# Rotary attention and a SiLU feed-forward layer on one core: small steps on three engines, and a new order of the work

## The chip, the cores and the metric

The kernel runs on one NeuronCore of one Trainium2 chip. The metric is device time in microseconds (us), from the start to the end of one execution. The kernel before takes 629.87 us (median of 3 runs, 629.48 to 632.24).

## What is computed

```python
def _attn_ref(q, k, v):                       # 4 batches, 8 heads, 576 positions, 64 numbers each, float32
    q_rot, k_rot = rotate(q), rotate(k)       # rotary embedding with cos and sin of 576 x 32 angles
    scores = (1 / 8) * q_rot @ k_rot.T
    attn = softmax(scores)                    # per row, minus its maximum
    return attn @ v

def _moe_ref(x, w_in, w_out):                 # x: 2304 x 512; w_in: 512 x 2048; w_out: 2048 x 512
    h = x @ w_in
    return (h * sigmoid(h)) @ w_out
```

`x` is the output of the attention, with the eight heads side by side. The scores of batch 0 are computed in float32; almost everything else is split into two float16 parts, a high one and a low one, whose products TensorE adds up.

## The kernel before, in words

**Stages.** The work is cut into some 2,500 named parts. Attention goes by *slots* `S i` (144 of them): the scores of up to 128 query rows of one head against all 576 keys. A slot has matmuls into PSUM (`S`, L953 for the first 16 slots, L1072 and L1081 for the others), the row maximum on VectorE (`max`, L958, L1102, L1104, L1097), the exponential on ScalarE (`exp`, L961 or L1115), the reciprocal of its sum (`nr1`, L1129), the split into a high part (`hi`, by `part_hi`, L324 or L330) and a low part (`lo`, by `part_lo`, L336 or L339) and a transposing DMA. In the first 16 slots there is no split: TensorE transposes the exponentials back into the slot's own PSUM buffer (`ET`, L966) and an engine copies them out (`EV`, L973), which sets that PSUM buffer free. Batch 0's q and k come into the same PSUM buffers by TensorE transposes (`qP`, L479 to L489) and are copied out by `qE` (L501, or L324 on VectorE). Tag `s` has two such buffers, `s3` one more.

Then `pv` multiplies by v, and the result is x for one *unit* (256 tokens; eight units and a rest). The feed-forward layer goes in *steps* over one unit and one of eight pieces `i` of the 2048 hidden columns: `m1` (24 matmuls, L1238), `tanh` on ScalarE (L1250), `g` on VectorE (L1254), its split `gh` and `gl`, and `m2` (twice 6 matmuls, L1295). `m1` has one PSUM buffer, so the next `m1` waits for this `g`.

**Weights.** Piece `i` of w_in and w_out (`wld`, L777 and L783) lands as float32 in a place that is still free, among others in `ring`. Three rounding steps follow (`wT` L798, `wC` L803 or L805, `wX` L811), the sum of squares (`wtr`, L839 on ScalarE or L349 on TensorE, `wtd` L353, `wmm` L854), the scale, and the split (`whi`, `wlo`) into w16.

**Scales.** `add_scale` (L297) makes every scale in three VectorE instructions on a tile of 128 x 1, 2 or 5: `sc0` (L305) takes the exponent bits, `sc1` (L311) multiplies them into a power of two `inv`, and `sc2` (L317) is its reciprocal `s`. There are 36 scales: 8 of weights, 12 of q and k, 16 of v. `add_w_group` (L880) makes a group's constants for unit 0, which runs over the weights in three groups (2, 3 and 3 pieces) as they come in: `wgr`, with two or three products, a maximum and a reciprocal (L892 to L894), all on VectorE. `tanh` of unit 0 reads what it makes. `times` (L323) is the helper for a product.

**Order.** Nothing is scheduled by the machine: `ORDER` names every part by its number and gives the engine that runs it (`a` ScalarE, `d` VectorE, `p` GpSimd, `t` TensorE, `s` SP's DMA queue), and `Plan.run` (L180) issues them so. Each engine executes its instructions in that order, and an instruction that waits holds up all that stand behind it on its engine.

Of the kernel before, what the change touches and what calls it, by code (L numbers as in the profile page):

```python
# [11 lines left out]
I32 = mybir.dt.int32  # L12
# [26 lines left out]
3s 472s 474p 473a 2s 1s 4s 9p 10p 475d 478a 468s 469a 11t 0d 6d 12d 5p 7t 8a 470d 471d 476a 663t 664d 673t 665a 479d  # L39
13s 477d 480t 481d 482d 20s 22p 674d 675a 14t 15d 21p 23t 45s 24a 36s 61s 483d 676t 677a 666t 667a 38d 484a 52s 25p  # L40
678t 26d 679d 680a 37p 39t 46t 42p 486a 485d 27t 28a 41d 488s 47d 489a 681t 682a 40a 54d 62t 487d 490a 57p 63d 29s 43t
668t 669d 496s 683t 44a 19s 497a 492s 58p 30t 53p 35s 670a 671t 684d 685a 75s 672a 31d 68t 491d 500a 69d 494a 70d 493a
501d 498d 71d 16p 499d 32d 74s 495d 686t 18d 687a 502a 503d 64d 55t 34d 504t 688t 693t 73s 48a 50d 56a 505d 506d 507d
1875d 689d 514s 694d 76a 690a 698t 695a 691t 692a 510d 696t 699d 534s 516d 508p 59t 60d 700a 701t 77a 697d 78t 509d
708t 702a 515a 79d 84p 713t 709d 714d 703t 1878t 536a 535a 512a 511p 704d 710a 705a 652d 90p 711t 91p 92p 518s 715a
517d 706t 562s 712a 707a 520a 519a 1876t 723t 718t 724d 513p 716t 717a 719d 563a 564a 1877d 538s 521d 565d 66d 539a
85p 86p 1885t 524t 725a 540a 537d 726t 727a 541d 80d 1879d 522t 1880p 523d 542t 543d 525d 720a 1889d 721t 1881p 558s
526t 544a 527d 81d 545d 546t 547d 1882d 728t 722a 559a 554s 560p 528d 561d 738t 529d 555a 548d 556a 733t 1883t 729d
# [1361 lines left out]
```

## Time and profile before

| | |
|---|---|
| median of 3 runs | 629.87 us |
| the profiled execution | 631.0 us, of which span 629.2 us |
| PE busy | 595.4 us (95%) |
| DVE busy | 468.0 us (74%) |
| ACT busy | 401.2 us (64%) |
| POOL busy | 323.5 us (51%) |
| mean granted clock of TensorE | 0.972 of 2.4 GHz |

In the profile PE is TensorE, PEld its weight loads, DVE VectorE, ACT ScalarE, POOL GpSimd and SP the engine that issues most DMAs. The shares are averages over stages that differ: VectorE is at 74% of the span, but at 95% in the stage in which the last weights come in. So the profile is read stage by stage. A granted clock of 1.00 is 2.4 GHz and 0.50 is 1.2 GHz.

### The profile page before, as it was taken

What the parts mean: (1) busy time and instruction counts of PE and PEld (TensorE: products, weight loads), DVE (VectorE), ACT (ScalarE), POOL (GpSimd) and SP (SyncE); (2) the same over time, 40 slices, a digit from 0 to 9 for tenths busy, and PEclk for the clock granted to TensorE, in tenths of its full rate; (3) what the DMA queues carried; (4) which work ended last, traced back from release to release, by engine and by line L of the source; (5) the groups of instructions that cost most, each with busy time, mean ns of one, the idle gap of its engine ahead of it and who ended that gap; (6) DMA issues with size and microseconds to landing.
All of it is one profiled execution on the core that took longest, in us unless ns stands there. A gap on an engine that the chain in (4) does not pass through costs nothing. (4 is left out here: it accounts for less than half of the span.)

```text
span 629.2 us, 12529 instructions
## 1 busy us (share of the span) xinstructions
PE 595.4 (95%) x4484; PEld 396.9 (63%) x4484; DVE 468.0 (74%) x1062; ACT 401.2 (64%) x834; POOL 323.5 (51%) x304
## 2 busy tenths in 40 slices
PE   1879999889999999999999999999999999999997
PEld 1657675555566666666667666567566666666663
DVE  2747879999998998999899999898778765121222
ACT  2656979988978777777676578577655653221221
POOL 4635636545665674745747654567674443423210
PEclk9976969989999999999999999999999999999999
DMA  6677708899989969998985889798866576100101
GB/s 200 180 257 272 239 1 205 232 207 188 193 149 185 195 123 157 175 187 181 201 147 127 150 167 166 128 197 160 160 111 115 99 124 95 42 10 1 35 1 33
DMA packets 210670, 91.17 MB, mean 145 GB/s; under 512 B 188464, under 2 KB 194352, under 8 KB 210608
## 3 DMA queue, kind: packets, MB, share of 16 engines
q1 hardware_dynamic: 210288, 89.79, 68.7%
q10 hardware_dynamic: 320, 0.59, 0.5%
q8 instruction: 35, 0.57, 0.4%
q14 instruction: 27, 0.22, 0.1%
HBM read 36.73 MB, written 4.72 MB: 66 GB/s over the span
## 5 line engine op out<-in xcount | busy, mean ns | idle before, releaser
L1238 PEld LDWEIGHTS <-w_in 128*128 128x128 f16 x1728 | 167.3, 98 | 37.1 <-issue 7.5
L1238 PE MATMUL m<-xh,w_in 128*128 128x256 f16 x1024 | 180.2, 274 | 1.3 <-DVE g L1254 1.2
L1295 PE MATMUL m<-w_out,gh 128*128 128x512 f16 x576 | 171.5, 379 | 0.0
L1238 PE MATMUL m<-xl,w_in 128*128 128x256 f16 x512 | 140.3, 274 | 0.6 <-POOL xl L1043 0.5
L1115 ACT ACTIVATE e<-s,small 128x576 f32<-128x576 f32 x128 | 98.8, 773 | 41.6 <-DVE pn L336 9.8
L1295 PE MATMUL m<-w_out,gl 128*128 128x512 f16 x288 | 109.1, 379 | 0.0
L1254 DVE SCALAR_TENSOR_TENSOR g<-g,m 128x512 f32<-128x512 f32 x72 | 49.0, 680 | 71.0 <-ACT g L1250 42.2
L1295 PEld LDWEIGHTS <-gh 128*128 128x128 f16 x576 | 52.6, 99 | 54.9 <-issue 4.0
L336 DVE SCALAR_TENSOR_TENSOR pn<-e,small,pn 128x576 f16<-128x576 f32 x85 | 77.4, 914 | 7.3 <-POOL pn L324 3.6
L1250 ACT ACTIVATE g<-m,small 128x512 f32<-128x512 f32 x64 | 43.7, 682 | 49.8 <-PE m L1238 43.0
L324 POOL TENSOR_SCALAR e<-e,small 128x576 f32<-128x576 f32 x43 | 37.5, 872 | 57.5 <-ACT pn L330 25.0
L1081 PE MATMUL s<-Tk,Tq 128*128 128x512 f16 (+1 forms) x384 | 59.9, 286 | 0.7 <-ACT e L1115 0.7
L339 POOL TENSOR_TENSOR pn<-e,pn 128x576 f16<-128x576 f32 x43 | 58.5, 1360 | 3.6
L324 POOL TENSOR_SCALAR pn<-e,small 128x576 f16<-128x576 f32 x40 | 36.6, 914 | 46.2 <-DVE small L1129 31.0
L330 ACT ACTIVATE pn<-e,small 128x576 f16<-128x576 f32 x65 | 49.8, 768 | 16.4 <-DVE small L1129 8.4
L1183 PE MATMUL pv<-pt,vh 128*64 128x320 f16 (+1 forms) x504 | 54.1, 290 | 0.0
L1295 PEld LDWEIGHTS <-gl 128*128 128x128 f16 x288 | 28.1, 98 | 34.0
L1097 DVE TENSOR_SCALAR_CACHE_REDUCE s<-s,small 128x576 f32<-128x576 f32 x57 | 46.1, 815 | 2.4 <-PE s L1087 1.2
L336 DVE SCALAR_TENSOR_TENSOR gl<-g,small,gh 128x512 f16<-128x512 f32 x50 | 41.1, 823 | 5.6 <-ACT gh L330 3.7
L1081 PEld LDWEIGHTS <-Tq 128*128 128x128 f16 x384 | 28.7, 100 | 25.3 <-issue 2.9
L1104 DVE TENSOR_REDUCE small<-s 128x1 f32<-128x576 f32 x51 | 38.0, 747 | 5.4 <-PE s L1081 4.4
L330 ACT ACTIVATE gh<-g,small 128x512 f16<-128x512 f32 x44 | 31.5, 716 | 14.5 <-DVE g L1254 13.1
(205 smaller groups left out, 1030.9 us busy)
## 6 DMA issues: line engine op xcount, KB each, us to landing
w_out<-in_moe_w_out_dram SPq DMA_DIRECT2D x4, 1024.0 KB, 7.6
w_in<-in_moe_w_in_dram SPq DMA_DIRECT2D x4, 1024.0 KB, 6.1
out_dram<-ob SPq DMA_DIRECT2D x28, 128.0 KB, 2.4
io<-in_q_dram SPq DMA_DIRECT2D x12, 288.0 KB, 3.3
io<-in_k_dram SPq DMA_DIRECT2D x12, 288.0 KB, 3.6
io<-in_v_dram SPq DMA_DIRECT2D x12, 288.0 KB, 4.0
io<-in_v_dram SPq DMA_DIRECT2D x13, 256.0 KB, 4.4
ring<-in_moe_w_in_dram SPq DMA_DIRECT2D x3, 1024.0 KB, 7.8
```

The source lines that it names most:

```text
L324: e.tensor_scalar(out=out, in0=in0, scalar1=s1, scalar2=s2, op0=ALU.mult, op1=ALU.bypass if s2 is None else ALU.mult)
L330: act.activation(hi, src, AF.Copy, scale=s)
L336: dve.scalar_tensor_tensor(out=lo, in0=src, scalar=s, in1=hi, op0=ALU.mult, op1=ALU.subtract)
L339: e.tensor_tensor(out=lo, in0=src, in1=hi, op=ALU.subtract)
L1081: pe.matmul(o, tq[:, j, 2 * c:2 * c + 2, :], kt[:, r0:r1, js], start=(n == 0), stop=(n == 1))
L1097: dve.tensor_scalar(out=t, in0=t, scalar1=cc[1], scalar2=None, op0=ALU.mult, op1=ALU.min, accum_out=m_of(1, 2),)
L1115: act.activation(buf("e", i), buf("s", i)[:, 0:S], AF.Exp, bias=m_of(1, 2), scale=-1.0 if fused[i] else cc[0], accum_out=m_of(2, 3),)
L1183: pe.matmul(o[64 * j:64 * j + 64, 0:m], vt[part][:, j, s, :], pt[:, a, j, 0:m], start=(z == 0), stop=(z == len(steps) - 1),)
L1238: pe.matmul(t[:, c, 0:n], w[:, wz, kk, fs], xx[:, kk, 0:n], start=(kk == 0 and x == 0), stop=(kk == KD - 1 and x == 2),)
L1250: act.activation(g[:, :, 0:n], t[:, :, 0:n], AF.Tanh, scale=th_v[units[u][0]][:, i:i + 1])
L1254: dve.scalar_tensor_tensor(out=g, in0=g, scalar=1.0, in1=t, op0=ALU.add, op1=ALU.mult)
L1295: pe.matmul(o, gs[gz][:, c, ts], w[:, wz, c], start=(first and c == 0 and x == 0), stop=(last and c == 1 and x == 2),)
```

## The change

Four edits:

- `sc1` may run on VectorE or GpSimd, `sc2` on VectorE, GpSimd or ScalarE, `wgr` on VectorE or GpSimd.
- The reciprocals of powers of two in `sc2` and `wgr` become integer arithmetic on the bits: 254 x 2^23 minus the bits (`flip`). The maximum in `wgr` becomes a two-operand instruction on GpSimd.
- `ORDER` is another table. By engine: of 36 `sc1`, 17 are on VectorE and 19 on GpSimd; of 36 `sc2`, 11 on VectorE, 14 on GpSimd, 11 on ScalarE; all three `wgr` on GpSimd, six instructions each. Larger parts change engine too, among them `rope` (rotary products, 53 on GpSimd and 35 on VectorE before, 39 and 49 now), `lo` (43 on GpSimd and 85 on VectorE before, 35 and 93 now), `hi` (65 on ScalarE, 40 on GpSimd, 23 on VectorE before, 75, 31 and 22 now) and `xh` (24 on ScalarE, 6 on VectorE, 2 on GpSimd before, 17, 14 and 1 now).
- Every part is still there once; TensorE's count of matmuls is the same.

```diff
 ORDER = """
-3s 472s 474p 473a 2s 1s 4s 9p 10p 475d 478a 468s 469a 11t 0d 6d 12d 5p 7t 8a 470d 471d 476a 663t 664d 673t 665a 479d
...
 """
-        def f1():
-            dve.tensor_scalar(
+        def f1(e):
+            eng[e].tensor_scalar(
                 out=inv, in0=live["bits", it].bitcast(F32), scalar1=2.0 ** 50, scalar2=2.0 ** -70,
                 op0=ALU.mult, op1=ALU.max,
             )
-        def f2():
-            dve.reciprocal(out=s, in_=inv)
+        def f2(e):
+            flip(e, s, inv)
         add("sc0", key, "d", f0, deps, list(bufs) + [bb], it)
-        add("sc1", key, "d", f1, [("sc0",) + key], [bb], it)
-        return add("sc2", key, "d", f2, [("sc1",) + key], (), it)
+        add("sc1", key, "dp", f1, [("sc0",) + key], [bb], it)
+        return add("sc2", key, "dpa", f2, [("sc1",) + key], (), it)
+
+    def flip(e, out, in_):
+        o, x, c = out.bitcast(I32), in_.bitcast(I32), float(254 << 23)
+        if e == "a":
+            act.activation(o, x, AF.Copy, scale=-1.0, bias=c)
+        else:
+            eng[e].tensor_scalar(out=o, in0=x, scalar1=-1.0, scalar2=c, op0=ALU.mult, op1=ALU.add)
...
-        def f():
-            times(dve, th_v[0][:, ii], inv_w[:, ii, 0], vn[0]["inv"], 2.0 ** -9)
+        def f(e):
+            e_ = eng[e]
+            times(e_, th_v[0][:, ii], inv_w[:, ii, 0], vn[0]["inv"], 2.0 ** -9)
...
-                dve.tensor_tensor(out=r, in0=inv_w[:, ii, 0], in1=inv_w[:, ii, 1], op=ALU.mult)
-                dve.reduce_max(out=r_g, in_=r, axis=AX.X)
-                dve.reciprocal(out=t, in_=r_g)
-                times(dve, alpha_g[:, ii], r, t, 2.0 ** -16)
-            times(dve, c_st[:, z:z + 1], r_g, vn[0]["inv"], 0.5)
-        add("wgr", (z,), "d", f, ...)
+                e_.tensor_tensor(out=r, in0=inv_w[:, ii, 0], in1=inv_w[:, ii, 1], op=ALU.mult)
+                if e == "d":
+                    e_.tensor_reduce(out=r_g, in_=r, axis=AX.X, op=ALU.max)
+                else:
+                    e_.tensor_scalar(
+                        out=r_g, in0=r[:, 0:1], scalar1=r[:, 1:2], scalar2=r[:, n - 1:n], op0=ALU.max, op1=ALU.max
+                    )
+                flip(e, t, r_g)
+                times(e_, alpha_g[:, ii], r, t, 2.0 ** -16)
+            times(e_, c_st[:, z:z + 1], r_g, vn[0]["inv"], 0.5)
+        add("wgr", (z,), "dp", f, ...)
```

**ScalarE, early in the program.** `pt<-s` is an `EV`, `Tk<-s` and `Tq<-s3` are `qE`, and `ring<-ring` is the rounding of a piece of the weights that has just landed. Line numbers after the change are up to 14 higher. Before:

```order
L501 ACTIVATE Tq_360<-s3_347 128x576
L798 ACTIVATE ring_133<-ring_133 128x1024
L973 ACTIVATE pt_284<-s_308 128x5x128
L501 ACTIVATE Tk_375<-s_322 128x576
L803 ACTIVATE ring_133<-ring_133 128x1024
```

With the change:

```order
L975 ACTIVATE e_343,small_118<-s_319,small_118 128x576
L509 ACTIVATE Tk_365<-s_352 128x576
L811 ACTIVATE ring_133<-ring_133 128x1024
L987 ACTIVATE pt_292<-s_319 128x5x128
L806 ACTIVATE ring_133<-ring_133 128x1024
```

Before, the copies out of both `s` buffers (`pt<-s_308`, `Tk<-s_322`) stand behind the instruction that waits for the ring's load; now `Tk<-s_352` stands ahead of it and only `pt<-s_319` behind it.

**TensorE, at the same place.** `s_410` and `s_454` are slot 1, `s_416` and `s_421` slot 4; `pv<-w_out` are matmuls for v's sum of squares. Before:

```order
L489 MATMUL s3_397<-id_t_125,n_341 64x128
L489 MATMUL s3_397<-id_t_125,rt_362 64x128
L953 MATMUL s_410<-Tk_203,Tq_184 128x64 x2
L953 MATMUL s_410<-Tk_203,Tq_184 128x448
L953 MATMUL s_416<-Tk_266,Tq_360 128x64 x2
L953 MATMUL s_416<-Tk_266,Tq_360 128x448
L349 LDWEIGHTS w_out_120
```

With the change:

```order
L497 MATMUL s3_403<-id_t_125,n_374 64x128
L497 MATMUL s3_403<-id_t_125,rt_394 64x128
L967 MATMUL s_421<-Tk_290,Tq_367 128x64 x2
L967 MATMUL s_421<-Tk_290,Tq_367 128x448
L357 LDWEIGHTS w_out_120
```

Slot 4 has moved ahead of slot 1, and v's five matmuls between them; slot 4 takes the buffer that `Tk<-s_352` frees.

**SP, the first issues.** Before:

```order
L423 DMA id_t_125<-in_ident_dram 128x128
L783 DMA w_out_120<-in_moe_w_out_dram 128x2x1024
L412 DMA cos_t_123<-in_cos_dram 128x128 x2
L414 DMA cos_t_123<-in_cos_dram 64x32 x2
L412 DMA sin_t_124<-in_sin_dram 128x256 x2
L414 DMA sin_t_124<-in_sin_dram 64x64 x2
L440 DMA w_in_119<-in_q_dram 128x2x256
```

With the change:

```order
L785 DMA w_in_119<-in_moe_w_in_dram 128x4x512
L448 DMA w_in_119<-in_q_dram 128x2x256
L453 DMA w_in_119<-in_q_dram 64x64 x2
L448 DMA w_in_119<-in_k_dram 128x2x256
L453 DMA w_in_119<-in_k_dram 64x64 x2
L420 DMA sin_t_124<-in_sin_dram 128x256 x2
L422 DMA sin_t_124<-in_sin_dram 64x64 x2
L431 DMA id_t_125<-in_ident_dram 128x128
L420 DMA cos_t_123<-in_cos_dram 128x128 x2
L422 DMA cos_t_123<-in_cos_dram 64x32 x2
L791 DMA w_out_120<-in_moe_w_out_dram 128x2x1024
```

The first piece of w_out has moved from the second place to behind q, k, sin, the identity and cos.

## Rows read from the trace of the kernel before

**Rows 1.** The page: the span, and the busy time of each engine.

```profile
span 629.2 us, 12529 instructions
PE 595.4 (95%) x4484; PEld 396.9 (63%) x4484; DVE 468.0 (74%) x1062; ACT 401.2 (64%) x834; POOL 323.5 (51%) x304
```

**Rows 2.** Busy time by stage; PEclk is the granted clock; last DMA share, GB/s.

```profile
0.00:38.00 38.00, 17.68 (x122) 13.84 (x123) 18.06 (x34) 15.80 (x23) 22.07 (x38) 1.00 0.72 215
38.00:58.50 20.50, 20.43 (x79) 15.74 (x79) 12.69 (x26) 13.34 (x28) 5.88 (x6) 0.50 0.60 209
58.50:79.00 20.50, 19.73 (x149) 14.27 (x148) 15.53 (x35) 19.48 (x33) 12.88 (x11) 1.00 0.83 273
79.00:89.30 10.30, 10.30 (x44) 8.26 (x45) 6.56 (x18) 6.80 (x13) 2.53 (x3) 0.50 0.01 2
...
99.40:165.70 66.30, 61.19 (x410) 37.39 (x406) 63.34 (x144) 58.27 (x110) 35.94 (x29) 0.97 0.90 202
165.70:578.80 413.10, 410.70 (x3314) 271.95 (x3313) 329.08 (x771) 267.39 (x579) 232.11 (x208) 1.00 0.76 139
578.80:629.20 50.40, 45.70 (x306) 29.65 (x304) 13.73 (x21) 10.56 (x34) 8.45 (x10) 0.99 0.09 22
```

**Rows 3.** The waits of PE up to 166 us: total, times, longest (us).

```profile
PE s L479 <- POOL n L465: 13.7, 1, 13.7
PE s L953 <- ACT pt L973: 3.5, 2, 3.3
...
PE pv L666 <- DVE small L305: 1.5, 1, 1.5
```

**Rows 4.** The timeline at 29 to 43 us, of SP's queue, ACT and PE.

```profile
29.32 1.38 SPq L777 DMA_DIRECT2D ring<-in_moe_w_in_dram  x1
...
36.02 1.12 ACT L798 ACTIVATE ring<-ring 128x1024 f32<-128x1024 f32 x1 [4.92 <-DMA ring<-in_moe_w_in_dram]
37.03 0.69 ACT L973 ACTIVATE pt<-s 128x640 f32<-128x640 f32 x1
...
37.78 4.84 PE L953 MATMUL s<-Tk,Tq 64*128 64x64 f32 x12 [3.32 <-ACT pt L973]
```

**Rows 5.** The timeline of the first two weight issues and the first use of w_out.

```profile
1.18 0.42 SPq L783 DMA_DIRECT2D w_out<-in_moe_w_out_dram  x1
...
6.82 1.15 ACT L798 ACTIVATE w_out<-w_out 128x1024 f32<-128x1024 f32 x1 [4.80 <-DMA w_out<-in_moe_w_out_dram]
...
10.91 0.59 SPq L777 DMA_DIRECT2D w_in<-in_moe_w_in_dram  x1
```

**Rows 6.** Groups of small instructions: count, busy us, mean ns, idle before.

```profile
L311 DVE TENSOR_SCALAR small<-small 128x2 f32<-128x2 f32 (+2 forms) x36 | 8.2, 231 | 0.4
L317 DVE RECIPROCAL small<-small 128x2 f32<-128x2 f32 (+2 forms) x36 | 5.8, 160 | 0.5
L1122 ACT ACTIVATE small<-small 128x1 f32<-128x1 f32 x69 | 13.4, 197 | 0.9
L1385 POOL MEMSET const-float32-1.0<- 128x1 f32 x1 | 0.1, 99 | 0.0
L467 POOL TENSOR_TENSOR rt<-w_in,sin_t 128x64 f32<-128x64 f32 x3 | 1.0, 321 | 0.0
```

**Rows 7.** The timeline of `wgr` on DVE: its first and its last instruction.

```profile
104.93 0.22 DVE L324 TENSOR_SCALAR small<-small 128x3 f32<-128x3 f32 x1
...
105.64 0.34 DVE L324 TENSOR_SCALAR small<-small 128x3 f32<-128x3 f32 x2
```

**Rows 8.** Instructions that write `pn`: duration in ns, least, median, largest.

```profile
L336 DVE SCALAR_TENSOR_TENSOR pn<-e,small,pn x85: 794/815/2035, 101.6 to 525.5; 128x576 f16<-128x576 f32 x85
...
L324 POOL TENSOR_SCALAR pn<-e,small x40: 739/748/1877, 103.3 to 523.5; 128x576 f16<-128x576 f32 x40
```

**Rows 9.** Groups of the `rope` products on POOL and on DVE.

```profile
L561 POOL TENSOR_TENSOR rt<-io,sin_t 128x576 f32<-128x576 f32 x15 | 24.7, 1656 | 8.8 <-DVE io L568 3.2 <-DMA io<-in_k_dram 3.0 <-PE s L489 1.4
...
L568 DVE TENSOR_TENSOR io<-io,rt 128x576 f32<-128x576 f32 x11 | 9.3, 848 | 0.0
```

More of the change, by code (lines that the diff above doesn't have):

```diff
@@ L44 @@
[L44 to L48, printed above, removed]
@@ new lines @@
+2352a 2345t 1778d 1754d 1755d 1779a 1780d 2346a 1703s 2353d 1771a 1781d 1741D 1758t 1759d 2348t 1756p 1742a 2358t
+1757s 1743a 2354p 1782d 1783d 2355p 1785t 1786d 2359a 2360d 1787a 1744a 1772d 1745d 2349a 1975t 2365t 2361a 1976d
+1760a 1746p 1747d 1761a 1784s 1773a 1803t 1748s 2362p 2356t 2357t 1762a 1763d 1977d 2366a 1788a 2367d 1804D 1774p
+1775s 1794t 2372t 1805d 1764d 2350s 1765d 1789d 1766s 1795d 1796a 1806a 1790d 1791a 1792d 1793s 1807a 1808d 1830t
+2363t 2364t 2368p 1797a 2369p 1831D 2373a 1798d 1799d 1809a 1810p 1800d 1811s 1821t 1822D 1823d 1832a 1833a 1848t
@@ new lines @@
+2370t 1978t 1824a 1849D 2374d 1801p 1825d 1826d 2375a 1827d 1828p 1979a 1866t 1850a 1851a 2379t 1867D 1868a 2376d
+1852a 1802s 1869a 1853d 1829s 1854d 2380a 1855p 1870d 1871d 1856s 1872a 1812t 1873p 2371t 1874s 1839t 1813d 1814d
+1815a 1816a 2381d 1840d 2382p 2377t 2378t 1841a 1817d 1834a 1818d 1819d 1835d 1857t 1858D 1820s 1859a 2383d 1836a
+2386t 1860a 1861d 1837d 2387a 1838s 1842a 1843d 2388d 2389a 1844d 1980d 2347s 2390d 1862d 2384t 1845a 1863p 2385t
+1864d 2393t 1846p 2394a 2391t 2395d 2392t 2396p 2397d 1981t 2400t 1865s 1982d 1983d 2401a 1847s 2402d 1984t 1985a
@@ L885, in add_w_group @@
         r, r_g, t = sm(n), sm(1), sm(1)
-        def f():
-            times(dve, th_v[0][:, ii], inv_w[:, ii, 0], vn[0]["inv"], 2.0 ** -9)
+        def f(e):
+            e_ = eng[e]
+            times(e_, th_v[0][:, ii], inv_w[:, ii, 0], vn[0]["inv"], 2.0 ** -9)
             if n == 1:
-                times(dve, r_g, inv_w[:, ii, 0], inv_w[:, i0, 1:2], None)
+                times(e_, r_g, inv_w[:, ii, 0], inv_w[:, i0, 1:2], None)
             else:
-                dve.tensor_tensor(out=r, in0=inv_w[:, ii, 0], in1=inv_w[:, ii, 1], op=ALU.mult)
-                dve.reduce_max(out=r_g, in_=r, axis=AX.X)
-                dve.reciprocal(out=t, in_=r_g)
-                times(dve, alpha_g[:, ii], r, t, 2.0 ** -16)
-            times(dve, c_st[:, z:z + 1], r_g, vn[0]["inv"], 0.5)
-        add("wgr", (z,), "d", f, [("sc1", "w", i) for i in range(i0, i0 + n)] + [("sc1", "vs", 0)], ())
+                e_.tensor_tensor(out=r, in0=inv_w[:, ii, 0], in1=inv_w[:, ii, 1], op=ALU.mult)
[8 more added lines that the diff above has]
+            times(e_, c_st[:, z:z + 1], r_g, vn[0]["inv"], 0.5)
+        add("wgr", (z,), "dp", f, [("sc1", "w", i) for i in range(i0, i0 + n)] + [("sc1", "vs", 0)], ())
     def add_w_all():
```

226 lines of the change are left out of this document (111 added, 115 removed).

## The prediction

> **What bounds the kernel now.** I read the page first [rows 1]: TensorE is busy for 595.4 of 629.2 us, so at most 34 us can come from filling its gaps; the other engines have room over the whole span. A share over the whole span hides the stages, so I cut the span by what TensorE does and read the busy time of each piece [rows 2]. From 165.7 to 578.8 us TensorE is busy for 410.7 of 413.1 us at the full clock: that stretch is bound by matmuls, and nothing that another engine saves there can be seen. The idle time lies ahead: 20.3 us up to 38 us (38.0 minus 17.68), 5.1 us in the stage in which the last weights come in (99.4 to 165.7), and 4.7 us at the end. In the weights' stage VectorE is busy for 63.3 of 66.3 us, 95%, and ScalarE for 58.3: there three engines are nearly full at once.
>
> A second loss is not in the busy time. From 38 to 58.5 us and from 79 to 89.3 us the granted clock is 0.50, that is 1.2 GHz [rows 2], and TensorE is busy throughout. 30.8 us of its time do the work of 15.4.
>
> Then I read what TensorE waited for [rows 3]. 13.7 us is the first load of q with its rotary product. The next is 3.3 us in one piece, for an `EV` on ScalarE. The timeline shows why [rows 4]: ScalarE sat for 4.92 us before an instruction on a piece of the weights whose load into `ring` had been issued at 29.32 us; it ran at 36.02 us, the `EV` behind it at 37.03, and TensorE went on at 37.78 with slots 1 and 4. Small steps of VectorE appear once among TensorE's waits, 1.5 us, and that one ends at `sc0` (L305), which stays where it is.
>
> **The change, part by part.** The profiled execution took 631.0 us, 1.8 us more than its span; the median of the runs shown is 1.1 us below it. I sum against 631.0 and take off 1.1 at the end.
>
> *Small steps.* VectorE gives away 19 `sc1` at 0.231 us, 4.4 us; 25 `sc2` at 0.160, 4.0 us [rows 6]; and three `wgr` of 1.05 us (104.93 to 105.98 us [rows 7]), 3.2 us: 11.6 us together, of which seven `sc1`, seven `sc2` and two `wgr`, 4.8 us, lie in the weights' stage. ScalarE takes 11 at 0.197 us, 2.2 us. GpSimd takes 19 + 14 + 18 = 51 instructions. The trace has no such instruction there. It has a memset of one column at 0.099 us and a two-operand product of 64 columns at 0.321 us [rows 6]; these are my bounds, 5.0 to 16.4 us. I take 0.2 us, nearest to ScalarE's 0.197 for the same shape: 10.2 us, on an engine that is idle for 305.7 us [rows 1]. On the path I count zero, because TensorE waits for none of them. The cover is TensorE's own queue of work; if that is gone, the price is that of rival 3.
>
> A row speaks against putting them on GpSimd: its split instruction takes 748 ns in the median and up to 1877 ns [rows 8], so something stretches it by up to 1.13 us. The Trainium skill (GPSIMD Engine Reference, section Key points) says that GpSimd shares its memory interfaces with VectorE and that two-operand VectorE instructions contend with it. By that rule a small step on GpSimd would be slow just where VectorE is full; the spread in the rows agrees, but no row here shows a small step there, and the sum keeps its 0.2 us.
>
> *Larger parts.* The new order does not leave VectorE lighter. It gives it 14 `rope` products at 0.85 us, 11.9 us, which took 1.66 us each on GpSimd [rows 9], and eight `lo` at 0.815 us, 6.5 us [rows 8]; `xh`, `gh` and the outputs move about evenly. 11.9 + 6.5 - 11.6 makes 6.8 us more on VectorE. In the weights' stage itself, by the places of the parts in the two tables, VectorE loses the 4.8 us and gets some eight larger parts more at about 0.7 us, 5.6 us. So that stage stays as full as it was: zero, between -4.8 us (the relief becomes time; TensorE's 5.1 us of idleness allow it) and +5.6 us (rival 3). In the stretch from 165.7 us VectorE is at 329 of 413 us; with all 6.8 us more it would be at 81%: zero, between -2.4 us (all of TensorE's idle time) and nothing that a row shows.
>
> *The start.* Here the order matters. The copy that frees the other `s` buffer now stands ahead of the instruction that waits for the ring's load, and slot 4 goes first and needs only that. So slot 4 runs in the 3.32 us in which TensorE waited. The two slots took 4.84 us at 1.2 GHz [rows 4]; half of it, 2.4 us, leaves the queue that starts at 37.78 us. `EV` itself, and slot 1 behind it, still wait for the ring's load. That gives -2.4 us. The ends: -3.3 us, if the whole wait goes, and +0.4 us, because SP has one weight issue more (0.42 us [rows 5]) ahead of the ring's load. The first piece of w_out is issued second before, at 1.18 us, and used at 6.82 [rows 5]. Now it follows q, k, sin and cos, at about the 10.91 us at which SP had finished the same set, so it is used near 16.5 us, and two `qE` on ScalarE stand behind it. What comes later by this has the 4.92 us of idle time before the ring's load as its cover, so I count zero; without that cover it would cost up to the 4 us between 17.7 (16.5 plus the instruction's 1.15) and 13.7 us, TensorE's first start.
>
> *The end.* TensorE's sequence there is the same. One low part goes to GpSimd, at least 0.75 us [rows 8], beside matmuls: zero.
>
> The sum: 631.0 - 2.4 = 628.6 us for an execution like the profiled one, 627.5 us as a median.
>
> **The rivals.**
> 1. *The clock stays up.* The fall at 38 us comes right behind the 3.32 us gap. If slot 4 in the gap keeps the clock at 2.4 GHz, TensorE's 20.4 us up to 58.5 us need 10.2; ScalarE is busy for 13.3 us there, so the stretch shrinks by 20.5 - 13.3 = 7.2 us at most, less 1.2 us, the half of slot 4's gain that a full clock takes back: 6.0, that is 621.5 us. Against it: the clock also fell at 79 us, behind a stretch in which TensorE was busy for 19.73 of 20.50 us [rows 2]. The Trainium skill (TensorE: Matmul & The Clock Gate, section Why this matters for your kernels) gives idle gaps between bursts as what lets the clock fall. By that rule the first low stretch would go with the gap and the time be this rival's; the trace agrees at 38 us and not at 79 us. Chance 0.12.
> 2. *VectorE's relief becomes time.* If the larger parts that refill the weights' stage are not urgent, 4.8 us come off: 622.7 us. For it: VectorE at 95% beside 5.1 us of TensorE's idleness. Against: ScalarE gets more there too. Chance 0.17.
> 3. *The small steps come late on GpSimd.* The scales of pieces 5, 6 and 7 now pass through GpSimd, where each stands behind a split instruction of up to 1.88 us [rows 8]; nothing of that piece can be split before. Three times 1.88 is 5.6 us: 633.1 us. It decides from the point at which TensorE has no other slot ready when `m1` or `m2` of such a piece is due. For it: nearly full engines. Against: GpSimd is idle for 30 of these 66 us [rows 2]. Chance 0.13.
> 4. *The clock falls once more.* In the weights' stage the mean granted clock is 0.97, some 4 us at half rate. A stretch there as long as the first, 20.5 us with TensorE busy for 92%, costs 9.4 us, less the 1.8 us that the present one costs: 7.6 us, 635.1 us. Chance 0.10.
> 5. *Nothing moves.* The steps do change engine, as the order shows, but the ring's load comes later by what slot 4 gains: 629.9 us. Chance 0.12.
>
> **How the numbers follow.** My forecast keeps 0.36, with 625 to 630 us of its own. Half a percent, about what a measurement of this kernel can tell from no change, is 3.1 us, so faster means below 626.7 us and slower above 633.0. A third of the forecast's chance, 0.12, lies below 626.7. Faster: 0.12 + 0.12 + 0.17 = 0.41. Same: 0.24 + 0.12 = 0.36. Slower: 0.13 + 0.10 = 0.23. The range goes from 619 us, rivals 1 or 2 with 2.4 us or so of the long stretch's idle time on top, to 636.5 us, rival 4 with 1.4 us to spare; what lies beyond is rivals 1 and 2 together, or 3 and 4.
>
> **What would show it.** Right: one slot's matmuls (L967) before the `EV` that waits for the ring's load, and TensorE reaching the first `m1` some 2 us before 99.4 us; VectorE still above 93% in the weights' stage; the 51 small steps on GpSimd near 0.2 us; the stretch after 165.7 us as full as now. Wrong: granted clock 1.00 between 38 and 58 us (rival 1); the weights' stage shorter than 63 us (rival 2), or longer than 69 us with TensorE waiting for split weights (rival 3); a new stretch at 0.50 behind 100 us (rival 4); small steps on GpSimd of half a microsecond and more; or new idle time of several us behind 165.7 us, which would say that VectorE's 6.8 us more are not hidden.

## The result, and the profile after

The changed kernel takes 621.98 us (median of 6 runs, 620.01 to 624.72) beside 630.04 us for the kernel before (6 runs): ratio 0.9896, 95% interval 0.986 to 0.9932. In a second comparison, with 12 runs beside 28, it was 624.68 against 628.32 us: 0.9935, 0.9911 to 0.996. So it is faster, by 8 us in the one and by 4 in the other. The forecast was 627.5.

The profiled execution took 620.01 us. Its page, span and busy times, against [rows 1]:

```profile
span 618.2 us, 12511 instructions
PE 589.8 (95%) x4484; PEld 391.4 (63%) x4484; DVE 471.3 (76%) x1039; ACT 403.9 (65%) x845; POOL 295.5 (48%) x306
```

VectorE is not lighter: 3.3 us more than before. GpSimd is, by 28 us. Then the busy time by stage: first the same cuts as in [rows 2], then cuts at the first `m1` (91.3 us), at the seventh (155.1; before 165.7) and behind the last of the full stretch; the columns are the same.

```profile
0.00:38.00 38.00, 23.62 (x141) 18.34 (x142) 20.12 (x51) 15.15 (x22) 12.61 (x22) 0.91 0.74 228
38.00:58.50 20.50, 18.99 (x114) 14.08 (x115) 17.93 (x35) 17.99 (x37) 14.45 (x20) 0.92 0.82 281
58.50:79.00 20.50, 18.38 (x143) 14.11 (x143) 19.02 (x33) 18.45 (x32) 14.70 (x14) 1.00 0.52 171
79.00:89.30 10.30, 9.32 (x66) 5.41 (x68) 8.49 (x21) 9.22 (x18) 6.83 (x10) 1.00 0.32 88
91.30:155.10 63.80, 60.55 (x400) 37.38 (x400) 61.55 (x112) 59.21 (x117) 34.24 (x35) 0.97 1.00 205
155.10:567.80 412.70, 411.05 (x3312) 271.21 (x3311) 329.88 (x768) 269.86 (x586) 202.46 (x196) 1.00 0.75 138
567.80:618.20 50.40, 45.86 (x308) 29.86 (x306) 12.30 (x18) 12.72 (x37) 8.79 (x10) 1.00 0.12 27
```

Of the 11.0 us between the two spans, 8.1 lie ahead of the first `m1` (91.29 us instead of 99.43), 2.5 in the weights' stage (63.8 us instead of 66.3), and 0.4 in all the rest, which is as full as it was. From 38 to 89 us the granted clock is 0.92 and 1.00 where it was 0.50 for 30.8 us; and from 38 to 79 us VectorE is busy for 36.95 of 41 us, 90%, where it was for 28.22, 69%. What TensorE waited for, up to the first steps of the feed-forward layer, against [rows 3]:

```profile
PE s L487 <- DVE n L473: 13.1, 1, 13.1
PE m L1252 <- DVE g L1268: 1.8, 2, 1.6
PE s L980 <- ACT e L975: 1.6, 4, 0.5
PE s L967 <- DVE pt L989: 1.5, 1, 1.5
PE mx L357 <- DVE w_out L819: 1.3, 1, 1.3
```

The 3.3 us ahead of slots 1 and 4 are gone. The timeline of ScalarE and TensorE shows the same place as [rows 4]:

```profile
33.51 0.66 ACT L509 ACTIVATE Tk<-s 128x576 f32<-128x576 f32 x1
35.79 1.16 ACT L811 ACTIVATE ring<-ring 128x1024 int32<-128x1024 uint16 x1 [1.62 <-DMA ring<-in_moe_w_in_dram]
35.99 1.46 PE L967 MATMUL s<-Tk,Tq 64*128 64x64 f32 x6
36.85 0.69 ACT L987 ACTIVATE pt<-s 128x640 f32<-128x640 f32 x1
37.77 1.46 PE L967 MATMUL s<-Tk,Tq 64*128 64x64 f32 x6
```

Slot 4 runs at 35.99 us, beside the instruction on the ring's load, and slot 1 at 37.77, both at 2.4 GHz: 1.46 us each, not 4.84 for the two.

The small steps, by groups (count, busy us, mean ns, idle before), against [rows 6], and the spread of one of them (least, median, largest in ns):

```profile
L311 POOL TENSOR_SCALAR small<-small 128x2 f32<-128x2 f32 (+1 forms) x19 | 10.1, 532 | 29.1 <-DVE small L305 26.9 <-DVE small L1138 1.2 <-DVE small L1143 0.2
L329 POOL TENSOR_SCALAR small<-small 128x2 int32<-128x2 int32 (+2 forms) x17 | 8.6, 505 | 8.6 <-DVE small L311 4.3 <-PE mx L1024 2.5 <-DVE small L1143 0.8
L905 POOL TENSOR_SCALAR small<-small 128x1 f32<-128x1 f32 x3 | 1.9, 622 | 0.3
...
L329 DVE TENSOR_SCALAR small<-small 128x2 int32<-128x2 int32 x6 | 2.4, 401 | 0.2
L329 DVE TENSOR_SCALAR small<-small 128x1 int32<-128x1 int32 x5 | 0.7, 149 | 0.2
...
L327 ACT ACTIVATE small<-small 128x1 int32<-128x1 int32 (+1 forms) x11 | 2.1, 194 | 2.3 <-DVE small L311 2.3
...
L329 POOL TENSOR_SCALAR small<-small x17: 192/308/1151, 25.3 to 452.4; 128x2 int32<-128x2 int32 x9, 128x1 int32<-128x1 int32 x7, 128x5 int32<-128x5 int32 x1
```

On GpSimd the 51 take 25 us (10.1, 8.6, 1.9 and, not shown, 3.4 for nine products by a constant and 1.1 for three of two operands), 0.49 us each. On ScalarE they cost what was expected: 194 ns each, against 197.

**A caution on the two profiles.** Each run gives its mean granted clock; twice its distance from 1, times the span, is its time at 1.2 GHz behind the first rise. The profile of before had 34.8 us of it and that of after 13.6. But 79 runs of the kernel before, on three chips, had 25.5, 22.8 and 27.9 us in the mean, and within one chip the time of a run goes with it: a line through those runs rises by 0.27, 0.25 and 0.16 us for each us at 1.2 GHz. So the profile before was an execution with much of it, and by such a line 3.4 to 5.7 us of the 11.0 (21.2 us times 0.16 to 0.27) go with the clock. Between the kernels on one chip the difference is 27.9 against 18.7 us: 1.5 to 2.5 us by the same lines. This is an estimate: the lines show what goes together, not which causes which.

### The profile page after: what moved, and what is told of

Same layout as the page of the kernel before. It is cut to its first block, busy times and chain, and to the rows that moved or that the text cites. A ratio compares the mean times of both kernels' runs of the same rounds, so it can differ in the third digit from the quotient of the medians.

```text
span 618.2 us, 12511 instructions
## 1 busy us (share of the span) xinstructions
PE 589.8 (95%) x4484; PEld 391.4 (63%) x4484; DVE 471.3 (76%) x1039; ACT 403.9 (65%) x845; POOL 295.5 (48%) x306
## 4 chain that ended last, share of the span: by engine, by line
PE 79%; DVE 7%; ACT 5%; DMA 4%; issue 2%; POOL 1%; SPq 1%; POOLq 0%; DVEq 0%; ACTq 0%
PE m L1309 28%; PE m L1252 27%; PE pv L1197 7%; PE s L1095 7%; DMA pt<-pn 2%; PE s L1086 2%; PE s L967 1%; PE s L1101 1%; PE s L980 1%; DMA w_in<-in_q_dram 1%; DMA w_out<-in_moe_w_out_dram 1%; PE mx L1034 1%; ACT e L1129 1%; PE s L487 1%; PE s L357 1%
## 5 line engine op out<-in xcount | busy, mean ns | idle before, releaser
L344 DVE SCALAR_TENSOR_TENSOR pn<-e,small,pn 128x576 f16<-128x576 f32 x93 | 82.2, 887 | 6.9 <-ACT pn L338 4.1
L338 ACT ACTIVATE pn<-e,small 128x576 f16<-128x576 f32 x75 | 57.3, 768 | 15.8 <-DVE small L1143 12.4
L1095 PE MATMUL s<-Tk,Tq 128*128 128x512 f16 (+1 forms) x384 | 61.4, 286 | 0.6 <-ACT e L1129 0.5
L332 POOL TENSOR_SCALAR pn<-e,small 128x576 f16<-128x576 f32 x31 | 27.0, 871 | 56.5 <-DVE small L1143 38.1
L1111 DVE TENSOR_SCALAR_CACHE_REDUCE s<-s,small 128x576 f32<-128x576 f32 x59 | 47.9, 817 | 6.2 <-PE s L1095 4.2
L344 DVE SCALAR_TENSOR_TENSOR gl<-g,small,gh 128x512 f16<-128x512 f32 x53 | 43.1, 813 | 11.8 <-ACT gh L338 7.4
L347 POOL TENSOR_TENSOR pn<-e,pn 128x576 f16<-128x576 f32 x35 | 45.5, 1300 | 2.9
L332 POOL TENSOR_SCALAR g<-g,small 128x512 f32<-128x512 f32 x19 | 17.0, 894 | 56.4 <-ACT gh L338 37.9
L332 POOL TENSOR_SCALAR e<-e,small 128x576 f32<-128x576 f32 x35 | 28.3, 809 | 30.6 <-ACT pn L338 23.2
```

Source lines behind the costliest of these rows:

```text
L332: e.tensor_scalar(out=out, in0=in0, scalar1=s1, scalar2=s2, op0=ALU.mult, op1=ALU.bypass if s2 is None else ALU.mult)
L338: act.activation(hi, src, AF.Copy, scale=s)
L344: dve.scalar_tensor_tensor(out=lo, in0=src, scalar=s, in1=hi, op0=ALU.mult, op1=ALU.subtract)
L347: e.tensor_tensor(out=lo, in0=src, in1=hi, op=ALU.subtract)
L1095: pe.matmul(o, tq[:, j, 2 * c:2 * c + 2, :], kt[:, r0:r1, js], start=(n == 0), stop=(n == 1))
L1111: dve.tensor_scalar(out=t, in0=t, scalar1=cc[1], scalar2=None, op0=ALU.mult, op1=ALU.min, accum_out=m_of(1, 2),)
```

## The experiments

The theory to begin with: the gain is the new order ahead of the first `m1`, most of it through the clock. The rivals: VectorE's relief of small steps is the gain, in whatever order; or the small steps cost and the order gains more. The runs, each against the kernel before on its own chip (three chips, four kernels each); "low" is the mean time at 1.2 GHz of the runs, the kernel's and then before's; the last three columns are the profiled execution's first `m1`, the time from there to the ninth, and the rest of its span. In `prompt_dve`, `start_new`, `rest_new`, `recip_back` and `recip_fill` an `sc2` that runs on VectorE is a reciprocal, as in the kernel before.

| run | median us | ratio (interval) | low us | first m1 | to ninth | rest |
|---|---|---|---|---|---|---|
| before (profile) | | | | 99.4 | 82.2 | 447.5 |
| changed (profile) | 621.98 | 0.9896 (0.986 to 0.9932) | | 91.3 | 80.2 | 446.7 |
| order_alone | 641.41 | 1.0233 (1.0194 to 1.0273) | 34.4, 25.5 | 101.6 | 86.2 | 450.2 |
| steps_alone | 640.64 | 1.0207 (1.0163 to 1.025) | 36.4, 25.5 | 98.8 | 88.2 | 450.1 |
| gap_back | 626.12 | 0.9978 (0.9951 to 1.0006) | 27.1, 25.5 | 96.1 | 79.4 | 447.8 |
| fill_gap | 625.80 | 0.9966 (0.994 to 0.9991) | 15.2, 25.5 | 93.6 | 82.0 | 447.6 |
| prompt_dve | 633.50 | 1.0087 (1.0053 to 1.0122) | 25.0, 22.8 | 96.0 | 82.8 | 449.8 |
| start_new | 630.97 | 1.0038 (1.0006 to 1.007) | 25.7, 22.8 | 93.2 | 90.3 | 447.2 |
| rest_new | 629.31 | 1.0025 (0.9999 to 1.0052) | 33.1, 22.8 | 98.3 | 85.9 | 446.1 |
| slot4_first | 628.26 | 1.0016 (0.9991 to 1.0041) | 27.3, 22.8 | 94.1 | 82.6 | 447.7 |
| changed_again | 624.68 | 0.9935 (0.9911 to 0.996) | 18.7, 27.9 | 93.4 | 82.4 | 446.6 |
| recip_back | 623.78 | 0.9927 (0.9899 to 0.9954) | 20.7, 27.9 | 93.0 | 82.4 | 446.6 |
| steps_twice | 635.06 | 1.0099 (1.0067 to 1.0131) | 29.8, 27.9 | 98.0 | 85.1 | 449.9 |
| recip_fill | 623.89 | 0.9934 (0.9904 to 0.9963) | 18.2, 27.9 | 93.7 | 80.8 | 446.6 |

### Each half alone

The new table with the old small steps (`sc1`, `sc2` and `wgr` given the letter `d` at their places in the table, and the functions of the kernel before):

```diff
-ORDER of the change
+ORDER of the change, with every sc1, sc2 and wgr marked d
-        add("sc1", key, "dp", f1, [("sc0",) + key], [bb], it)
-        return add("sc2", key, "dpa", f2, [("sc1",) + key], (), it)
+        add("sc1", key, "d", f1, [("sc0",) + key], [bb], it)
+        return add("sc2", key, "d", f2, [("sc1",) + key], (), it)
```

> The new table of the order with the old small steps: all sc1, sc2 and wgr back on VectorE, with reciprocals as before. Theory (the gain is the order of the first 91 us, and most of it is the clock): 620.5 to 623.5 us, the first m1 within 1 us of 91.3 us, about 14 us at 0.50 after the first rise as in the changed kernel. Rival (VectorE's relief of the small steps is the gain): the 8 us go, 628 to 630 us. Between them (some 4 us each): 625 to 627 us.

The old table with the new small steps:

```diff
-ORDER of the change
+ORDER of the kernel before, with sc1, sc2 and wgr marked as in the change
```

> The old table with the new small steps: sc1, sc2 and wgr on the engines that the changed kernel gives them, integer arithmetic for the reciprocals, every other part at its old place on its old engine. Theory: 628.5 to 632 us, no change against the kernel before, first m1 near 99.4 us, the two low stretches of the clock at 38 and 79 us still there. Rival (VectorE's relief is the gain): 622 to 625 us. Second rival (small steps of half a microsecond on GpSimd are late): above 633 us.

Both are slower than the kernel before, by 2.3% and 2.1%, some 13 us. For `steps_alone` that is what its second rival expected (above 633 us); for `order_alone` no theory had it. The gains of the two halves don't add up: each table has places for its own small steps. The timeline of `order_alone` shows such a place (VectorE, ScalarE and GpSimd at the first weight scale):

```profile
25.64 0.16 DVE L310 TENSOR_SCALAR small<-small 128x2 f32<-128x2 f32 x1
...
28.09 0.76 DVE L323 TENSOR_SCALAR Tk<-s 128x576 f32<-128x576 f32 x1 [1.50 <-PE s L488]
29.23 0.83 DVE L974 COPY pt<-s 128x640 f32<-128x640 f32 x1 [0.38 <-PE s L965]
29.97 0.15 DVE L316 RECIPROCAL small<-small 128x2 f32<-128x2 f32 x1
...
30.16 1.21 ACT L329 ACTIVATE w_in<-w_in,small 128x1024 f16<-128x1024 f32 x1 [4.06 <-DVE small L316]
30.22 1.52 POOL L323 TENSOR_SCALAR w_out<-w_out,small 128x1024 f16<-128x1024 f32 x1 [7.10 <-DVE small L316]
```

and the same place in the changed kernel (GpSimd and ScalarE):

```profile
25.26 0.28 POOL L329 TENSOR_SCALAR small<-small 128x2 int32<-128x2 int32 x1 [2.42 <-DVE small L311]
...
25.58 1.22 ACT L338 ACTIVATE w_in<-w_in,small 128x1024 f16<-128x1024 f32 x1 [0.16 <-POOL small L329]
25.64 1.30 POOL L332 TENSOR_SCALAR w_out<-w_out,small 128x1024 f16<-128x1024 f32 x1
```

A reciprocal of 0.15 us, at a place made for another engine, stands behind rotary products (not shown), two waits and two copies of VectorE; the two split instructions on ScalarE and GpSimd begin 4.6 us later, and their queues with them. In `steps_alone` it is the other way round. Its page's busy times, ScalarE's wait on such a step, the group of `sc1` on GpSimd, and the low parts on VectorE, here and in the kernel before:

```profile
PE 595.9 (94%) x4484; PEld 395.7 (62%) x4484; DVE 469.3 (74%) x1000; ACT 401.5 (63%) x845; POOL 338.0 (53%) x355
...
ACT small L326 <- POOL small L310: 8.1, 3, 3.6
...
L310 POOL TENSOR_SCALAR small<-small 128x2 f32<-128x2 f32 (+1 forms) x19 | 10.3, 543 | 19.6 <-DVE small L304 18.6
...
L343 DVE SCALAR_TENSOR_TENSOR pn<-e,small,pn 128x576 f16<-128x576 f32 x85 | 80.6, 952 | 8.3 <-POOL pn L331 4.9
L336 DVE SCALAR_TENSOR_TENSOR pn<-e,small,pn 128x576 f16<-128x576 f32 x85 | 77.4, 914 | 7.3 <-POOL pn L324 3.6
```

ScalarE waits 8.1 us in three pieces for an `sc1` on GpSimd, and GpSimd 18.6 us for an `sc0`, with its own larger work behind it in the queue. And VectorE, which gave away the same steps as in the change, is busy for 469.3 us: no less than the 468.0 of [rows 1]. What it kept takes longer: the 85 low parts 952 ns each instead of 914, 3.2 us in all.

Both runs keep a table that was made for the other placing. No run gives the small steps away in the old order at places that fit them, so how much the relief would bring without the other parts of the new table stays open.

### The gap at 34 us and the clock

The changed kernel with the gap opened again, on ScalarE's queue:

```diff
 exp 3
-qE 0 2 k
 wC 1 in 0
 EV 3
+qE 0 2 k
 wT 1 in 0
```

> The changed kernel with one instruction moved on ScalarE: the copy qE of the other s buffer goes back behind the instruction that waits for the ring's load and behind EV, so slot 4 can't run before that load. TensorE then waits from about 36.0 to 37.5 us. If the gap ahead of 38 us is what lets the clock fall: granted clock 0.50 for some 10 to 20 us behind 38 us, 626 to 630 us. If the clock does not hang on this gap: only the 1.5 us of waiting come back, 622.5 to 624 us, and the clock stays as in the changed kernel.

The kernel before with the gap filled, ahead of slot 1:

```diff
+FILL = {1: 28}
...
+            if i in FILL:
+                d = pools["mx"].tile(TAGS["mx"][1], F32, tag="mx", name="mx")
+                for _ in range(FILL[i]):
+                    pe.matmul(d[:, 0:128], id_t, id_t, is_transpose=True, start=True, stop=True)
             for c0, c1, k0 in cols:
```

> The kernel before with 28 additional transposes of the identity into the free mx bank ahead of slot 1, about 0.107 us each at 2.4 GHz, 3.0 us: they lie in the 3.32 us in which TensorE waits for the ring's load, and move no work. Their results are not read. If that gap is what lets the clock fall at 38 us: granted clock 1.00 from 38 to 58 us, and 623 to 626 us with nothing else changed. If the clock falls anyway: 629 to 632 us.

The kernel before with the gap used for slot 4, as the change does, and nothing else moved (ScalarE, then TensorE):

```diff
+qE 0 2 k
 wT 1 in 0
 EV 3
-qE 0 2 k

+S 4
 S 1
-S 4
```

> The kernel before with two parts moved: the copy qE of the second s buffer ahead of the instruction that waits for the ring's load, and slot 4 ahead of slot 1. The prediction's term alone: slot 4's half of 4.84 us leaves the queue, 2.4 us, ratio 0.996. If the clock also stays up from 38 to 58 us, as it did with the gap filled: ratio 0.990 to 0.994. If the ring's load takes it back: 0.999 to 1.001.

The wait that `gap_back` opens, and the same window, 38 to 58.5 us, in `gap_back`, `fill_gap` and `slot4_first`:

```profile
37.42 1.46 PE L966 MATMUL s<-Tk,Tq 64*128 64x64 f32 x6 [1.15 <-ACT pt L986]
...
38.00:58.50 20.50, 20.43 (x89) 15.56 (x89) 14.89 (x28) 13.56 (x27) 10.73 (x18) 0.58 0.57 195
```

```profile
38.00:58.50 20.50, 18.21 (x113) 13.60 (x114) 18.12 (x32) 17.64 (x34) 9.43 (x7) 0.92 0.78 270
```

```profile
38.00:58.50 20.50, 18.83 (x85) 14.63 (x85) 13.88 (x27) 13.03 (x29) 6.02 (x5) 0.59 0.67 235
```

In the profiles, the gap does let the clock fall: opened in the changed kernel it brings 0.58 instead of 0.92, filled in the old one 0.92 instead of 0.50. The gap of 1.15 us costs 2.7 us against the ratio of `changed_again` (about 0.4 to 5.1 by the two intervals), 5.2 against that of the first comparison. The runs behind the profiles go the same way: 15.2 us at 1.2 GHz with the gap filled against 25.5 on the same chip, and 27.1 with it opened, where the changed kernel had 18.7 on another. The Trainium skill (TensorE: Matmul & The Clock Gate, section Why this matters for your kernels) names idle gaps between bursts as what lets it fall; these two runs agree. But the price was overrated. `fill_gap` has 10.3 us less at 1.2 GHz than the kernel before and gains 2.1 us (0.6 to 3.8), 0.2 us for each; the 6.0 us that rival 1 gave it are not there. Rival 1 looked for the next limit at ScalarE's 13.34 us; in the window at the full clock VectorE goes from 12.69 to 18.12 us of the 20.5, ScalarE to 17.64, and TensorE itself is busy for 18.21.

`slot4_first` is the term of the forecast by itself, and it gains nothing: 1.0 us slower, between 0.6 faster and 2.6 slower. Its timeline of TensorE, and of ScalarE at the ring's load:

```profile
34.07 1.46 PE L952 MATMUL s<-Tk,Tq 64*128 64x64 f32 x6
37.45 2.54 PE L952 MATMUL s<-Tk,Tq 64*128 64x64 f32 x6 [1.92 <-ACT pt L972]
...
35.69 1.12 ACT L797 ACTIVATE ring<-ring 128x1024 f32<-128x1024 f32 x1 [4.38 <-DMA ring<-in_moe_w_in_dram]
```

Slot 4 does run in the gap, as in the change; 1.92 us of waiting stay behind it, the clock falls at 38 us all the same, and the runs have no less time at 1.2 GHz than the kernel before (27.3 us in the mean, 22.8 before).

### VectorE's small steps at matched places

In `order_alone` the place of the steps and their engine were mixed. So: the changed kernel with each `sc1` and `sc2` on VectorE, right behind its `sc0`; `wgr` stays on GpSimd.

```diff
 sc0 w 0
+sc1 w 0 on VectorE
+sc2 w 0 on VectorE
...
-sc1 w 0
-sc2 w 0 on GpSimd
```

> The changed kernel with every sc1 and sc2 back on VectorE, but each right behind its sc0 (not, as in order_alone, at the place that the table had for another engine), sc2 as a reciprocal; wgr stays on GpSimd. Theory (order_alone lost because small steps stood behind larger work of VectorE, not because VectorE had more to do): ratio to the kernel before 0.985 to 0.993, as the changed kernel's 0.990, some 620 to 624 us where the kernel before takes 629. Rival (the 8.4 us that VectorE gives away are the gain): ratio 0.996 to 1.004.

The first weight scale is ready at 25.55 us (26.05 in `changed_again`), the second at 47.82 (47.91), so no scale need be late; and still the kernel takes 633.5 us: its ratio of 1.0087 is 0.0152 above that of `changed_again`, 9.5 us (about 6.8 to 12.2 by the two intervals). Its busy times, the wait of TensorE that grew from 1.5 us, and one behind 170 us that grew from 0.2:

```profile
PE 594.6 (95%) x4484; PEld 393.7 (63%) x4484; DVE 483.0 (77%) x1083; ACT 402.9 (64%) x834; POOL 281.8 (45%) x273
...
PE s L969 <- DVE pt L991: 3.5, 1, 3.5
...
PE s L1097 <- ACT e L1131: 2.2, 4, 1.0
```

VectorE has 12.3 us more than the 470.7 of `changed_again`: 9.2 of small steps by the groups, the rest in instructions that came out longer. In the new order that is on the path nearly one to one. In the two profiles, 6.3 us apart, it costs 2.6 us ahead of the first `m1`, 0.4 from there to the ninth and 3.2 behind it (449.8 against 446.6 us), in the stretch that the prediction called bound by matmuls. TensorE's waits behind 170 us add up to 2.9 us there, 0.4 in `changed_again`. The rival holds and more, the first theory falls: at both places that were tried for the small steps on VectorE, the new order is slower than the old one. The rest of what `order_alone` lost, from 1.0087 to 1.0233, is the places in VectorE's queue and the three `wgr` (1.05 us each in the kernel before); no run takes the two apart.

Whether the same holds in the old order, by doubling the cost there:

```diff
         def f1():
+          for _ in range(2):
             dve.tensor_scalar(
...
         def f2():
+            for _ in range(2):
-            dve.reciprocal(out=s, in_=inv)
+                dve.reciprocal(out=s, in_=inv)
```

> The kernel before with every sc1 and sc2 issued twice on VectorE, the second with the same result: 36 x (0.231 + 0.160) = 14.1 us more on VectorE. Theory (in the old order VectorE has room, so its small steps are hidden there, and giving them away alone can gain nothing): ratio 1.000 to 1.006, up to 4 us. Rival (they are on the path in the old order too): 8 to 14 us, ratio 1.013 to 1.023.

6.2 us (4.2 to 8.2) for 13.1 us more on VectorE (481.1 against 468.0): between the two expectations, half on the path. So the small steps were not hidden in the old order either. In the profiles the price lies from the first `m1` to the ninth (85.1 us instead of 82.2) and behind it (449.9 instead of 447.5). The doubling makes each scale 0.4 us later too, so the 6.2 us are the price of both.

### Parts of the table

The new table up to the first `m1`, then what is left in the old order; and the reverse.

```diff
-ORDER of the change
+ORDER of the change up to m1 0 0, then all other parts as they stand in the kernel before
```

> The new table up to the first m1, and from there all that is left in the old table's order on the old table's engines (small steps on VectorE again). Theory (the gain lies ahead of the first m1): first m1 near 91.3 us, ratio 0.986 to 0.992. Rival (the weights' stage with its relieved VectorE carries half or more): ratio 0.994 to 1.000 although the first m1 comes at 91 us.

```diff
-ORDER of the change
+ORDER of the kernel before up to m1 0 0, then all other parts as they stand in the change
```

> The reverse: the old table up to the first m1, from there the new table with the new engines of the small steps. Theory: first m1 near 99.4 us, ratio 0.997 to 1.003. Rival (the weights' stage carries half or more): ratio 0.990 to 0.995, the ninth m1 some 4 us earlier counted from the first.

Neither tells the halves apart. `rest_new` is in its theory's range, but with 33.1 us at 1.2 GHz where the kernel before had 22.8 on that chip, so what its order is worth doesn't show. In `start_new` the seam costs: the first `m1` comes at 93.2 us, as with the change, but the second 8.25 us later instead of 4.3:

```profile
101.46 0.37 PE L1254 MATMUL m<-xh,w_in 128*128 128x256 f16 x1 [4.18 <-DVE small L1140]
```

The two starts leave different parts done (slot 20's exponential in the one, slot 19's and a split piece of weights in the other), and the other table's queues have to make up for it; that this is what delays the second `m1` was not tested. `start_new` has only 2 of the change's 19 `sc1`, and 6 of its 25 `sc2`, off VectorE, so it lacks most of the relief too.

### The changed kernel again, and small repairs

> The changed kernel as it is, beside the kernel before on the chip of the other runs of this call. If its gain is the same here: ratio 0.986 to 0.993. If the gain was partly that of one chip or of lucky spells of the clock: 0.994 to 1.000.

Faster here too, by about 4 us. Its window from 38 us and its weights' stage (first to seventh `m1`):

```profile
38.00:58.50 20.50, 18.95 (x114) 14.14 (x113) 17.84 (x35) 18.18 (x37) 14.38 (x21) 0.92 0.79 272
...
93.40:159.40 66.00, 62.23 (x400) 38.14 (x400) 61.77 (x112) 59.66 (x117) 33.35 (x35) 0.95 0.93 199
```

The weights' stage takes 66.0 us in this execution, the 66.3 of before: the 2.5 us seen there in the first profile are not a lasting gain.

The integer form taken back where the step stays on VectorE:

```diff
         def f2(e):
-            flip(e, s, inv)
+            if e == "d":
+                dve.reciprocal(out=s, in_=inv)
+            else:
+                flip(e, s, inv)
```

> The changed kernel, but the eleven sc2 that stay on VectorE are reciprocals again (160 ns each before the change, against 401 ns for the integer form): 11 x 0.24 is 2.6 us less on VectorE, and nothing else. Theory (in the new order VectorE's small steps are on the path nearly one to one up to 165 us, as the 11.7 us of prompt_dve were): 1.5 to 3 us faster than the changed kernel of this call. Rival (VectorE's small steps are hidden, prompt_dve lost by something else): within 1 us of it.

0.9 us faster than `changed_again`, which the intervals can't tell from nothing. The expectation had the size wrong. The eleven took 3.1 us as integers (2.4 and 0.7 in the groups above) and 1.8 as reciprocals, so 1.3 us and not 2.6, and 1.2 of that is one instruction of 1367 ns beside a large product on GpSimd:

```profile
L329 DVE TENSOR_SCALAR small<-small x11: 138/155/1367, 47.2 to 437.5; 128x2 int32<-128x2 int32 x6, 128x1 int32<-128x1 int32 x5
```

In the median the integer form took 155 ns, no more than the reciprocal. So this run says little about VectorE's small steps. The same kernel with TensorE's wait at 18.4 us filled:

```diff
         def gram():
+            if not n_fill[0]:
+                n_fill[0] = 1
+                d = pools["mx"].tile(TAGS["mx"][1], F32, tag="mx", name="mx")
+                for _ in range(10):
+                    pe.matmul(d[:, 0:128], id_t, id_t, is_transpose=True, start=True, stop=True)
             for z, blk in enumerate(blocks()):
```

> recip_back with ten additional transposes of the identity (1.1 us at 2.4 GHz, results not read) in the 1.32 us in which TensorE waits at 18.4 us for the rounded piece of w_out. In the changed kernel the clock falls for 6.8 us behind that gap. If the gap is its cause: granted clock 1.00 from 18 to 41 us, and 1 to 2.5 us faster than recip_back. If not: the same time as recip_back within 1 us, the clock low near 21 us.

No difference: 623.89 and 623.78 us. Up to 38 us the clock is up (0.99, against 0.91 in `recip_back`), but then it falls for 10 us, behind a wait of 1.32 us for a load of v that `recip_back` does not have. The first two windows of `recip_fill`, and that wait:

```profile
0.00:38.00 38.00, 21.84 (x149) 16.57 (x149) 22.20 (x52) 14.72 (x22) 14.88 (x25) 0.99 0.74 229
38.00:58.50 20.50, 19.58 (x101) 14.83 (x100) 14.49 (x28) 15.90 (x33) 10.14 (x16) 0.77 0.68 234
...
36.92 0.29 PE L364 MATMUL pv<-w_out 128*128 128x128 bf16 x2 [1.32 <-DMA w_out<-in_v_dram]
```

That the filling kept the clock up ahead of 38 us is not shown: in the profile of `changed_again` TensorE has the same wait, 1.3 us, and the clock stays up there too.

So no version here is surely better than the change.

## Why the prediction was right or wrong

The direction and the range held; the sum behind them did not, and the forecast's own mechanism is not what made the kernel faster. That 627.5 us lies as near as it does is luck: two terms put at zero were wrong by more than the result, with opposite signs.

- **The start, -2.4 us.** The step's events came as described: slot 4 at 35.99 us ahead of the `EV`, no 3.3 us gap. Its price failed: alone, in `slot4_first`, it is worth nothing (+1.0 us, -0.6 to +2.6). "Half of 4.84 us leaves the queue" took a shorter queue for an earlier end. The first piece of w_out did come at 16.57 us, as foreseen, with a wait of 1.3 us for TensorE behind it that the sum had put at zero.
- **Small steps, 0 on the path.** This is the step that failed most. "TensorE waits for none of them" is true of the waits' last link, but an instruction that is on no wait of TensorE still takes time from a queue whose other work TensorE waits for. Measured: 9.5 us (6.8 to 12.2) for the `sc1` and `sc2` on VectorE in the new order, 6.2 us for 13.1 us in the old. It also answers "nothing that another engine saves there can be seen", of the stretch from 165.7 us: in the profiles 3.2 and 2.4 us of these prices lie behind the ninth `m1`.
- **Larger parts, 0.** The second failed zero, of the opposite sign: with these small steps still on VectorE the new table is 5.5 us slower than the old one (`prompt_dve`, 3.3 to 7.6). It loads VectorE from 38 us on (36.95 us of 41, not 28.22), and the relief pays for it: +5.5 - 9.5 = -4.0 us, which is the ratio of `changed_again` again, since the 9.5 us were read against it.
- **GpSimd's price, 0.2 us each.** It is 0.49, above the upper bound of 0.321. "Nearest to ScalarE's" was the wrong row: the spread of the split instruction on GpSimd, which the prediction named, was the right one. The rule on the shared memory interfaces that stood beside it (the Trainium skill, GPSIMD Engine Reference, section Key points) agrees with the trace: 192 ns at the least, 1151 at the most, in the same kernel. Each of the 23 steps that took more than 0.55 us ran for at least 0.53 us beside a two-operand instruction of VectorE; but nine steps of under 0.31 us ran beside one for nearly all their time too, so that is not the whole of it. That the price costs no time in the change is likely, since GpSimd has 28 us less to do there, but no run shows it by itself.
- **Rival 1, the clock.** Its cause agrees with `fill_gap` and `gap_back`, and it happened in part: 0.92 from 38 to 58.5 us. Its time, 621.5, looks like a hit on the first comparison's 621.98, but the 6.0 us were wrong: some 2 us.
- **Rival 2, VectorE's relief becomes time.** Nearest to what the runs show, but its place was wrong: the weights' stage took 63.8 and 66.0 us in two executions, before 66.3. By `prompt_dve` the relief counts at the start, where the new order puts more on VectorE, and behind the ninth `m1`; only in the old order, by `steps_twice`, does it count in between.
- **Rival 3, small steps late on GpSimd.** Not in the change; with the old table such waits do appear (`steps_alone`, +13 us; how much of it is theirs no run separates).
- **Rivals 4 and 5** did not come: behind 100 us the clock is low for 3.4 and 6.8 us in the two profiles, not for 20, and the time moved.
- **What was to be shown:** VectorE above 93% in the weights' stage holds (61.55 of 63.8), as does the full stretch behind it.
- **The base.** The sum started from one profiled execution as the kernel's normal course. It had 34.8 us at 1.2 GHz, where the means on three chips are 23 to 28: the low stretches from which rival 1 was priced were longer than usual.

What stays open: which places of the new table make up for its load on VectorE, and how much the relief would bring in the old order at fitting places. The change wins 4 us as a whole, and the two hybrids do not take it apart. Also why the gain was 8 us in the one comparison and 4 in the other; their intervals overlap.

## What to carry to other kernels

An instruction that no one is seen to wait for is free only if its queue has room there: price it by doubling it in place, which costs one run and gave 6.2 us here where the waits said zero. Where order and engines are written out by hand they are one object: a part given to another engine at an unchanged place stands behind other work, and half a change can be slower (2.3% and 2.1%) though the whole is faster. And before pricing a clock stretch from one profile, compare its mean clock with that of the other runs.

## What the runs showed of the hardware that was not expected

- Small work on GpSimd has no fixed price: steps on one to five columns took from 0.19 to 1.15 us, 0.49 in the mean over the 51, against 0.19 on ScalarE.
- On VectorE a small step's price depends on its form and on GpSimd. In the kernel before, eight of the 22 `TENSOR_SCALAR` from `small` to `small` on two columns took more than 0.25 us, up to 1.34, each beside an instruction of GpSimd; none of the 124 on one column took more than 0.22, and none of the 172 reciprocals more than 0.18. The 401 ns of the six integer steps on two columns are such a mean: 155 to 169 ns for three, 265, 282 and 1367 for the three beside GpSimd. Reciprocals at the same places, by the groups of `recip_back`:

```profile
L317 DVE RECIPROCAL small<-small 128x2 f32<-128x2 f32 x6 | 1.0, 158 | 0.2
L317 DVE RECIPROCAL small<-small 128x1 f32<-128x1 f32 x5 | 0.8, 160 | 0.2
```

- Work taken off VectorE and put on GpSimd can come back as longer instructions: in `steps_alone` VectorE gave away its small steps and was as busy as before, with its low parts at 952 ns instead of 914.
- 1 us at 1.2 GHz went with 0.16 to 0.27 us of time in this kernel, over the runs of one and the same program, and `fill_gap` gained 0.2 us for each; both are less than the half that TensorE's own work would say.
- Waits of TensorE of 1.15 us (`gap_back`) and 1.92 us (`slot4_first`) had a granted clock of 0.58 and 0.59 behind them, from 38 to 58.5 us. One of 1.3 us at 18.4 us had a fall behind it in the profile of the change (0.91 up to 38 us), and none in that of `changed_again`.
